# The last stores cut into shares of 117 and 11 rows, and four earlier stores into halves of 64 rows

## The chip, the cores and the metric

The kernel runs on one core of a Trainium2 chip. A core has five engines with instruction streams of their own: TensorE (PE in the profile) for matrix products, VectorE (DVE), ScalarE (ACT), GpSimd (POOL) and SyncE (SP), which issues transfers only. Data moves between the core's memory (SBUF, 128 rows called partitions) and DRAM on 16 DMA engines. The metric is the device time of one execution in microseconds, the median of several runs.

## What is computed

For 4 batches and 8 heads, keys and values are mixed over 8 blocks of 96 tokens by a matrix made doubly stochastic in five rounds; each block of queries then attends to its own mixed block. The result, 768 tokens by 512 features for each batch, goes through a gated network whose output is the kernel's output.

```python
for _ in range(5):                       # sort_net: [4, 8, 8, 8]
    P = np.exp(P - max); P /= rows(P); P /= cols(P)
k_sorted, v_sorted = P @ k_blocks, P @ v_blocks
x = softmax(q_b @ k_sorted.T / 8) @ v_sorted      # [4, 768, 512]
h = np.maximum(x @ w_in, 0.0)                     # 512 -> 1024
u, v = h[..., :512], h[..., 512:]
v_n = (v - mean) / sqrt(var + 1e-6)
v_s = einsum('ts,bsd->btd', w_spatial, v_n) + b_spatial[None, :, None]
out = (u * v_s) @ w_out                           # [4, 768, 512], float32
```

The output is 4 x 768 x 512 numbers of 4 bytes, 6.3 MB, and each batch has six tiles of 128 tokens (rows) by 512 columns.

## The kernel before

The work is cut into small units: one load, one group of matrix products with the instruction that takes the result out of PSUM, one store. The text `ORDER` (lines 18 to 51) names them one after another, and this order, written out by hand, is the order of the instructions on every engine; no scheduler moves them. A unit is a name with its arguments, and the function `u_` + name issues it. Stages of different batches are interleaved: while one batch is in its attention, the batch before it is in the gated network.

The units that matter here stand at the end of a batch.

- `OP:ps:b:n` multiplies the gated values by `w_out` for a pair of tiles, n and n+1 of batch b, into a PSUM tile (line 635). `OE:A` or `OE:D` copies the pair to a buffer `o_sb` in SBUF, on ACT (line 115) or DVE (line 117). `OS:b:n` stores the pair, 128 rows x 2 x 512, in one DMA on SP's queue (line 650).
- The last batch, b = 3, ends in smaller steps. `SH` and `GH` make the spatial product and the gate in pieces of 512 and 256 tokens (lines 665 to 678). `OH:ps:3:n:c0:c1` is the last product for one tile n and columns c0 to c1 (line 685), `OI` copies it to SBUF, and `OJ:3:n:c0:c1:S` stores it on SP's queue, or with `A` on ACT's (line 697). Tiles 2, 3, 1 and 0 are whole (512 columns), tiles 4 and 5 in column halves of 256.
- `XD:3:0` is a DMA transpose on SP's queue (line 506). It turns the first half of batch 3's attention output, and the products of line 597 read it.
- `XD`, `OS` and `OJ` on SP's queue go out in the order of the text: SP issues a DMA when its inputs are ready, and what stands behind it in the text waits.

Before the change batch 3's stores are, in the order of the text: tiles 2, 3, 4 (left half) on SP; 5 (left half) on ACT; 5 and 4 (right halves) on SP; 1 on ACT; 0 on SP. Of the earlier pairs, 1:2 and 1:4 (batch 1, tiles 2 and 4) are stored just ahead of `XD:3:0`, and 2:4, 1:0, 2:0 and 0:4 while batch 3's spatial product runs.

Copies and stores share 8 buffers (pool `ld`): a copy into a buffer waits until the store that read it last has landed. In the built program the DMAs of SP and ACT also take their completion semaphores from a set of eight, and a DMA is issued only once the DMA before it on the same semaphore has landed. The end of the program (line 807) waits for all DMAs, and then for all engines.

Of the kernel before, what the change touches and what calls it, by code (L numbers as in the profile page):

```python
# [38 lines left out]
VP:3:A:2:2:3 AT:1:3:3:1 GT:P:1:0 VP:2:A:2:0:1 ST:2:3 AT:1:3:2:1 AT:3:3:1:1 UP:0:A:2:1:1 OP:1:1:0 ST:2:0 ST:2:1 ST:2:2  # L39
OE:A:1:0 AT:2:3:0:1 LN:2:0:6 LA:2:1 UP:0:D:2:0:0 SC:1:3:0:0 LA:2:3 SC:3:3:1:0 LA:2:2 LA:2:5 LA:2:0 OP:2:1:4 AT:1:3:0:0  # L40
AT:3:3:1:0 XD:3:1 OE:A:1:4 OP:0:1:2 LA:2:4 SC:1:3:3:0 OE:D:1:2 SC:3:3:2:0 SP:2:2:2 AT:1:3:2:0 UP:0:A:2:0:1 AT:3:3:3:0
CK VP:2:A:3:4:5 GT:D:2:2 OS:1:2 SP:1:2:1 ST:3:5 OS:1:4 XD:3:0 SP:3:2:3 SP:2:2:0 ST:3:4 CF:3 GT:D:2:1 GT:P:2:3
UP:0:A:3:1:0 VP:2:D:3:2:3 VP:3:A:3:0:1 ST:3:0 ST:3:1 ST:3:2 UP:2:A:3:0:1 GT:P:2:0 LF OP:1:2:2 ST:3:3 OE:A:2:2 LN:3:0:6
OP:0:2:0 LA:3:4 LA:3:5 OS:2:2 OE:A:2:0 UP:3:D:3:1:1 LA:3:2 LA:3:0 OP:2:2:4 LA:3:3 OE:A:2:4 LA:3:1 OS:2:4 UP:0:A:3:0:0
SH:1:3:3:0 GH:P:3:3:0 SH:2:3:0:0 GH:D:3:0:0 SH:0:3:1:0 SH:2:3:2:0 SH:3:3:1:1 GH:P:3:1:0 SH:1:3:0:1 GH:P:3:2:0 OS:1:0
GH:P:3:1:1 SH:2:3:3:1 SH:3:3:2:1 OH:1:3:2:0:512:0:4 OS:2:0 GH:P:3:0:1 GH:D:3:2:1 GH:D:3:3:1 OH:2:3:3:0:512:0:4 OS:0:4
OH:0:3:4:0:256:0:4 OI:A:3:2:0:512 OI:A:3:3:0:512 OH:3:3:5:0:256:0:4 OI:D:3:4:0:256 OI:D:3:5:0:256 OJ:3:2:0:512:S
OJ:3:3:0:512:S OJ:3:4:0:256:S OJ:3:5:0:256:A OH:2:3:5:256:512:0:4 OH:1:3:1:0:512:0:4 OH:3:3:4:256:512:0:4
OI:D:3:5:256:512 OI:A:3:1:0:512 OJ:3:5:256:512:S OI:A:3:4:256:512 OJ:3:4:256:512:S OJ:3:1:0:512:A OH:2:3:0:0:512:0:4
OI:A:3:0:0:512 OJ:3:0:0:512:S  # L50
"""


# [12 lines left out]
def kernel(  # L66
# [12 lines left out]
    nc = tc.nc  # L79

    B, H, S, D = q.shape
    NB = sort_net.shape[-1]
    BLK = S // NB
    G = S // 128
# [23 lines left out]
    def queue(eng):  # L108
        if "general" in st:
            return nc.gpsimd  # L110
        return nc.scalar if eng == "A" else nc.sync

    def copy(eng, out, in_):
        if eng == "A":
            nc.scalar.copy(out=out, in_=in_)  # L115
        else:
            nc.vector.tensor_copy(out=out, in_=in_)  # L117
# [37 lines left out]
    st = {}  # L155
    count = {"e": 0, "k": 0}

    def ld_tile(name):
        return ld.tile([128, H, G * D], BF16, name=name, tag="ld")
# [197 lines left out]
    def u_QP(eng, b, hp):  # L357

        b, hp = int(b), int(hp)
        if ("qp", b) not in st:  # L360
            st["qp", b] = ld_tile("qp").rearrange("p h c -> p (h c)").rearrange(
                "p (k g h d) -> p k g h d", k=HP, g=G, h=2)
        getattr(nc, {"P": "gpsimd", "D": "vector"}[eng]).tensor_copy(
            out=st["qp", b][:, hp].rearrange("p g h d -> p h g d"),
            in_=st["q", b][:, 2 * hp:2 * hp + 2].rearrange("p h (g d) -> p h g d", g=G),
        )

    def u_QX(b, lo, hi):
# [326 lines left out]
    def u_OJ(b, n, c0, c1, eng="S"):  # L695
        b, n, c0, c1 = (int(x) for x in (b, n, c0, c1))
        queue(eng).dma_start(out=out[b, n * 128:(n + 1) * 128, c0:c1], in_=st["o1", b, n, c0])

    def u_CK():
        nc.vector.memset(bad, 0.0)  # L700
        over = lambda col, rows, in_, op, bound, test: (
            nc.vector.tensor_reduce(out=ends[0:rows, col:col + 1], in_=in_, axis=AX.X, op=op),
            nc.vector.tensor_scalar(
                out=bad[0:rows, col:col + 1], in0=ends[0:rows, col:col + 1],
                scalar1=bound, scalar2=None, op0=test),
        )
        recs = rec_all.rearrange("p n h i -> p (n h i)")
        over(0, BLK, recs, ALU.max, 1.0 / SUM_LO, ALU.is_gt)
        over(1, BLK, recs, ALU.min, 1.0 / SUM_HI, ALU.is_lt)
        over(2, BH, first[:, 0:NB], ALU.max, SUM_HI, ALU.is_gt)  # L710
        over(3, BH, first[:, 0:NB], ALU.min, SUM_LO, ALU.is_lt)
        over(4, BH, first[:, NB:2 * NB], ALU.min, COL_LO, ALU.is_lt)
# [99 lines left out]
```

## Time and profile before

| | before |
|---|---|
| median of 3 runs | 157.69 us (157.53 to 157.9) |
| the profiled execution's own time | 158.23 us |
| its span, first to last instruction | 156.4 us |
| PE busy | 147.1 us, 94% |
| DVE, ACT, POOL busy | 77%, 52%, 24% |
| granted TensorE clock | 0.999 |
| last matrix product ends | about 151.6 us into the span |

The profile gives times from the start of the span. "x" is a count of instructions. In rows of the timeline the first two numbers are start and duration; "SPq" and "ACTq" are the two engines' sequencers, which issue transfers. In a table of windows the columns are the stretch, its length, then busy time and count for PE, weight loads, DVE, ACT and POOL, then the granted clock, the mean busy share of the 16 DMA engines (1/16 is 0.06), and GB/s. A row of DMA issues gives the size and the median time from issue to landing.

### The profile page before, as it was taken

The numbers are of one execution on the slowest core, as the hardware profiler recorded it, in microseconds if no ns is written. First come the engines' busy times: TensorE is split into PE (matmuls) and PEld (weight loads), VectorE is DVE, ScalarE is ACT, GpSimd is POOL, SyncE is SP. The second block draws the span as 40 slices with busy tenths as digits, with TensorE's granted clock in tenths as the row PEclk, the third lists the DMA queues.
The fourth block names the chain that finished last, engine by engine and source line by source line (L and its number), as shares of the span: only waits on it lengthen the run. The fifth ranks groups of instructions, "written<-read, shape, count | busy, mean of one in ns | idle before, by whom it ended". The sixth has DMA issues, their size and how long they took to land.

```text
span 156.4 us, 3976 instructions
## 1 busy us (share of the span) xinstructions
PE 147.1 (94%) x1650; PEld 89.7 (57%) x1665; DVE 120.4 (77%) x270; ACT 81.5 (52%) x112; POOL 36.8 (24%) x43
## 2 busy tenths in 40 slices
PE   6998898989999999999999999999999999999970
PEld 2355776844686669557655465555565545555640
DVE  4778699849997798479898889899969796747530
ACT  3466898867889504876556034556443025540230
POOL 7923855624000040052000000400000340006500
PEclk9999999999999999999999999999999999999999
DMA  2999999999999999990026445600569300349082
GB/s 76 264 204 204 205 204 205 207 219 239 274 209 203 204 204 204 244 198 4 0 41 198 79 160 96 114 0 4 101 235 71 67 0 0 134 151 379 13 307 105
DMA packets 27653, 23.57 MB, mean 151 GB/s; under 512 B 7280, under 2 KB 24688, under 8 KB 27632
## 3 DMA queue, kind: packets, MB, share of 16 engines
q0 software_dynamic: 14352, 11.80, 47.6%
q1 hardware_dynamic: 12992, 11.10, 26.4%
q10 hardware_dynamic: 288, 0.39, 0.7%
q8 instruction: 14, 0.23, 0.6%
q14 instruction: 7, 0.06, 0.1%
HBM read 24.78 MB, written 6.29 MB: 199 GB/s over the span
## 4 chain that ended last, share of the span: by engine, by line
PE 91%; DVE 2%; ACT 2%; issue 1%; DVEq 0%; ACTq 0%
PE ps L609 15%; PE ps L597 14%; PE ps L554 13%; PE ps L635 10%; PE ps L226 7%; PE ps L488 5%; PE ps L665 5%; PE ps L442 4%; PE ps L383 4%; PE ps L314 4%; PE ps L685 3%; PE ps L410 2%; PE ps L518 2%; PE ps L531 1%; DVE kt L117 1%
## 5 line engine op out<-in xcount | busy, mean ns | idle before, releaser
L447 ACT ACTIVATE ex<-ps 96x768 bf16<-96x768 f32 x32 | 24.8, 805 | 8.7 <-PE ps L442 8.6
L625 POOL TENSOR_TENSOR gt<-z,u_sb 128x768 bf16<-128x768 f32 x6 | 9.8, 1641 | 79.0 <-DVE z L615 61.2
L609 PE MATMUL ps<-wspT,v_sb 128*128 128x384 bf16 x144 | 25.1, 326 | 0.0
L597 PE MATMUL ps<-xT,w_in_sb 128*128 128x384 bf16 x128 | 23.5, 326 | 0.0
L554 PE MATMUL ps<-w_in_sb,xT 128*128 128x512 bf16 x87 | 22.1, 380 | 1.2 <-issue 0.8
L496 DVE TENSOR_TENSOR x_sb<-ps,rec_all 96x512 bf16<-96x512 f32 x32 | 22.0, 687 | 1.1
L609 PEld LDWEIGHTS <-v_sb 128*128 128x128 bf16 x144 | 13.5, 98 | 8.9
L571 DVE BATCH_NORM_STATS2 stats<-v_sb 128x6 f32<-128x512 bf16 x24 | 16.3, 678 | 2.0 <-ACT v_sb L121 1.5
L115 ACT COPY o_sb<-ps 128x1024 f32<-128x1024 f32 (+2 forms) x12 | 9.7, 816 | 15.2 <-PE ps L685 10.2
L635 PE MATMUL ps<-w_out_sb,gt 128*128 128x512 bf16 x68 | 16.7, 379 | 0.2
L615 DVE TENSOR_TENSOR z<-ps,b_bc 128x768 f32<-128x768 f32 x12 | 11.4, 952 | 7.0 <-PE ps L609 6.8
L121 ACT ACTIVATE u_sb<-ps 128x768 bf16<-128x768 f32 x12 | 9.7, 810 | 13.1 <-PE ps L597 13.0
L597 PEld LDWEIGHTS <-w_in_sb 128*128 128x128 bf16 x128 | 11.6, 98 | 7.4
L554 PEld LDWEIGHTS <-xT 128*128 128x128 bf16 x96 | 8.6, 98 | 10.0 <-issue 1.0
L121 ACT ACTIVATE v_sb<-ps 128x1024 bf16<-128x1024 f32 (+1 forms) x9 | 8.8, 976 | 9.4 <-PE ps L554 9.4
L488 PEld LDWEIGHTS <-ex 96*128 96x128 bf16 x256 | 10.6, 97 | 3.5
L488 PE MATMUL ps<-vb,ex 96*128 96x65 bf16 x256 | 12.1, 193 | 0.0
L226 PE MATMUL ps<-warm 128*128 128x512 bf16 x35 | 10.6, 460 | 1.3 <-DVE warm L199 1.3
L635 PEld LDWEIGHTS <-gt 128*128 128x128 bf16 x72 | 6.7, 98 | 7.2
L115 ACT CAST kt<-ps 128x768 bf16<-128x768 f32 x9 | 6.9, 800 | 6.5 <-PE ps L383 6.5
L442 PE MATMUL ps<-qT,kt 64*128 64x96 bf16 x256 | 9.3, 204 | 0.5 <-DVE kt L117 0.4
L442 PEld LDWEIGHTS <-kt 64*128 64x128 bf16 x256 | 6.2, 94 | 5.8 <-issue 3.9
(94 smaller groups left out, 208.2 us busy)
## 6 DMA issues: line engine op xcount, KB each, us to landing
out_dram<-o_sb SPq DMA_DIRECT2D x9, 512.0 KB, 3.6
k_in<-in_k_dram POOLq DMA_DIRECT2D x4, 768.0 KB, 23.3
v_in<-in_v_dram POOLq DMA_DIRECT2D x4, 768.0 KB, 22.4
vb<-vm SPq DMA_DIRECT2D x24, 99.0 KB, 5.8
q_in<-in_q_dram POOLq DMA_DIRECT2D x3, 768.0 KB, 29.6
ws_in<-in_moe_w_spatial_dram POOLq DMA_DIRECT2D x2, 576.0 KB, 22.8
w_in_sb<-in_moe_w_in_dram POOLq DMA_DIRECT2D x2, 512.0 KB, 24.1
q<-in_q_dram SPq DMA_DIRECT2D x1, 768.0 KB, 4.6
```

Source lines behind the costliest of these rows:

```text
L115: nc.scalar.copy(out=out, in_=in_)
L121: nc.scalar.activation(out=out, in_=in_, func=AF.Relu)
L226: nc.tensor.matmul(t[:, 0, 0:int(w)], lhsT=warm[:, 0:128], rhs=warm[:, 0:int(w)], start=True, stop=True)
L442: nc.tensor.matmul(t[:, hh, 0:HW].rearrange("p (g x) -> p g x", g=G)[:, :, ii * TB:(ii + 1) * TB], lhsT=kT[rows, i * BLK:i * BLK + 128], r ...
L447: nc.scalar.activation(out=e_tile(b, hp, ih).rearrange("p h (x g) -> p h x g", g=G), in_=t[0:BLK, :, 0:HW].rearrange("p h (g x) -> p h x g ...
L488: nc.tensor.matmul(t[:, hh, ii * VW:ii * VW + D + 1], lhsT=e[:, c:c + 128], rhs=vb[b % 2][:, ih * NI + ii, 2 * hp + hh, 0:D + 1], start=Tr ...
L496: nc.vector.tensor_mul(out=x_sb[:, hp].rearrange("p i (h d) -> p h i d", h=2), in0=tv[:, :, :, 0:D], in1=_raw_ap(rec, 0, [rec.ap[0], [NI, ...
L554: nc.tensor.matmul(t[:, x, :], lhsT=st["xT", b][:, n // 3, kc, (n % 3) * 128:(n % 3 + 1) * 128], rhs=w_in_sb[:, kc, DH:DFF], start=(kc == ...
L571: nc.vector.bn_stats(out=stats, in_=st["v_sb", b, n])
L597: nc.tensor.matmul(t[:, x, 0:HW], lhsT=w_in_sb[:, kc, mc * 128:(mc + 1) * 128], rhs=st["xT", b][:, ih, kc, :], start=(kc == 0), stop=(kc = ...
L609: nc.tensor.matmul(t[:, x, 0:HW], lhsT=st["v_sb", b, n][:, mc * 128:(mc + 1) * 128], rhs=wspT[:, 3 * x:3 * x + 3, n, :], start=(n == 0), s ...
L635: nc.tensor.matmul(t[:, x, :], lhsT=st["gt", b, mc][:, (n0 + x) * 128:(n0 + x + 1) * 128], rhs=w_out_sb[:, mc, :], start=(mc == 0), stop=( ...
```

## The change

The matrix products, copies, loads and all other units stay as they are, and in the same order. Eight stores are cut by rows.

- `OT`, new, stores half the rows of a pair of tiles on SP's queue. The pairs 1:2, 1:4, 1:0 and 2:0 go out as rows 0 to 63 and then rows 64 to 127, at the places of their old `OS`.
- `OR`, new, stores some rows of a last tile. Tile 5 (left half, on ACT) and tile 4 (right half, on SP) go out as rows 0 to 116 and then rows 117 to 127, one behind the other on the queue they had. Of tile 1, rows 0 to 116 go out on ACT at the old place; of tile 0, rows 0 to 116 on SP at the old place, and then rows 117 to 127 of tile 0 and rows 117 to 127 of tile 1, both on ACT, end the text.
- Tiles 2 and 3, the left half of 4 and the right half of 5, and the pairs 2:2, 2:4 and 0:4, are stored as before.

In all, `out` is stored by 25 DMAs instead of 17: 20 on SP (15 before) and 5 on ACT (2 before). `u_QP`, which no unit of the text calls, is also rewritten.

```diff
-CK VP:2:A:3:4:5 GT:D:2:2 OS:1:2 SP:1:2:1 ST:3:5 OS:1:4 XD:3:0 ...
+CK VP:2:A:3:4:5 GT:D:2:2 OT:1:2:0:64 OT:1:2:64:128 SP:1:2:1 ST:3:5 OT:1:4:0:64 OT:1:4:64:128 XD:3:0 ...
...
-... GH:P:3:2:0 OS:1:0 GH:P:3:1:1 ... OS:2:0 GH:P:3:0:1 ...
+... GH:P:3:2:0 OT:1:0:0:64 OT:1:0:64:128 GH:P:3:1:1 ... OT:2:0:0:64 OT:2:0:64:128 GH:P:3:0:1 ...
...
-OJ:3:3:0:512:S OJ:3:4:0:256:S OJ:3:5:0:256:A OH:2:3:5:256:512:0:4 ...
+OJ:3:3:0:512:S OJ:3:4:0:256:S
+OR:3:5:0:256:A:0:117 OR:3:5:0:256:A:117:128 OH:2:3:5:256:512:0:4 ...
-OI:A:3:4:256:512 OJ:3:4:256:512:S OJ:3:1:0:512:A OH:2:3:0:0:512:0:4
-OI:A:3:0:0:512 OJ:3:0:0:512:S
+OI:A:3:4:256:512 OR:3:4:256:512:S:0:117 OR:3:4:256:512:S:117:128
+OR:3:1:0:512:A:0:117 OH:2:3:0:0:512:0:4 OI:A:3:0:0:512 OR:3:0:0:512:S:0:117 OR:3:0:0:512:A:117:128
+OR:3:1:0:512:A:117:128
...
+    def u_OT(b, n0, r0, r1):
+        b, n0, r0, r1 = (int(x) for x in (b, n0, r0, r1))
+        queue("S").dma_start(
+            out=out[b].rearrange("(c p) n -> p c n", p=128)[r0:r1, n0:n0 + 2, :], in_=st["o", b, n0][r0:r1])
+
+    def u_OR(b, n, c0, c1, eng, r0, r1):
+        b, n, c0, c1, r0, r1 = (int(x) for x in (b, n, c0, c1, r0, r1))
+        queue(eng).dma_start(out=out[b, n * 128 + r0:n * 128 + r1, c0:c1], in_=st["o1", b, n, c0][r0:r1])
```

More of the change, by code (lines that the diff above doesn't have):

```diff
@@ L41 @@
 AT:3:3:1:0 XD:3:1 OE:A:1:4 OP:0:1:2 LA:2:4 SC:1:3:3:0 OE:D:1:2 SC:3:3:2:0 SP:2:2:2 AT:1:3:2:0 UP:0:A:2:0:1 AT:3:3:3:0
[L42 to L49, printed above, removed]
-OI:A:3:0:0:512 OJ:3:0:0:512:S
+CK VP:2:A:3:4:5 GT:D:2:2 OT:1:2:0:64 OT:1:2:64:128 SP:1:2:1 ST:3:5 OT:1:4:0:64 OT:1:4:64:128 XD:3:0 SP:3:2:3 SP:2:2:0
+ST:3:4 CF:3 GT:D:2:1 GT:P:2:3 UP:0:A:3:1:0 VP:2:D:3:2:3 VP:3:A:3:0:1 ST:3:0 ST:3:1 ST:3:2 UP:2:A:3:0:1 GT:P:2:0 LF
+OP:1:2:2 ST:3:3 OE:A:2:2 LN:3:0:6 OP:0:2:0 LA:3:4 LA:3:5 OS:2:2 OE:A:2:0 UP:3:D:3:1:1 LA:3:2 LA:3:0 OP:2:2:4 LA:3:3
+OE:A:2:4 LA:3:1 OS:2:4 UP:0:A:3:0:0 SH:1:3:3:0 GH:P:3:3:0 SH:2:3:0:0 GH:D:3:0:0 SH:0:3:1:0 SH:2:3:2:0 SH:3:3:1:1
+GH:P:3:1:0 SH:1:3:0:1 GH:P:3:2:0 OT:1:0:0:64 OT:1:0:64:128 GH:P:3:1:1 SH:2:3:3:1 SH:3:3:2:1 OH:1:3:2:0:512:0:4
+OT:2:0:0:64 OT:2:0:64:128 GH:P:3:0:1 GH:D:3:2:1 GH:D:3:3:1 OH:2:3:3:0:512:0:4 OS:0:4 OH:0:3:4:0:256:0:4 OI:A:3:2:0:512
+OI:A:3:3:0:512 OH:3:3:5:0:256:0:4 OI:D:3:4:0:256 OI:D:3:5:0:256 OJ:3:2:0:512:S OJ:3:3:0:512:S OJ:3:4:0:256:S
+OR:3:5:0:256:A:0:117 OR:3:5:0:256:A:117:128 OH:2:3:5:256:512:0:4 OH:1:3:1:0:512:0:4 OH:3:3:4:256:512:0:4
+OI:D:3:5:256:512 OI:A:3:1:0:512 OJ:3:5:256:512:S OI:A:3:4:256:512 OR:3:4:256:512:S:0:117 OR:3:4:256:512:S:117:128
+OR:3:1:0:512:A:0:117 OH:2:3:0:0:512:0:4 OI:A:3:0:0:512 OR:3:0:0:512:S:0:117 OR:3:0:0:512:A:117:128
+OR:3:1:0:512:A:117:128
 """
@@ L362, in u_QP @@
                 "p (k g h d) -> p k g h d", k=HP, g=G, h=2)
-        getattr(nc, {"P": "gpsimd", "D": "vector"}[eng]).tensor_copy(
-            out=st["qp", b][:, hp].rearrange("p g h d -> p h g d"),
-            in_=st["q", b][:, 2 * hp:2 * hp + 2].rearrange("p h (g d) -> p h g d", g=G),
+        copy(
+            eng, st["qp", b][:, hp].rearrange("p g h d -> p h g d"),
+            st["q", b][:, 2 * hp:2 * hp + 2].rearrange("p h (g d) -> p h g d", g=G),
         )
```

## The prediction

> **What bounds the kernel now.** I began with the page's chain of work that ended last. TensorE carries it nearly throughout, and it ends in a copy of the last tile:
>
> ```profile
> PE 91%; DVE 2%; ACT 2%; issue 1%; DVEq 0%; ACTq 0%
> ...
> 146.62 4.95 PE ps L685 x30
> 151.56 0.02 issue
> 151.58 0.58 ACT o_sb L115
> ```
>
> The copy ends at 152.16, the span at 156.4. The change touches no product and no copy, so its place is mainly these 4.3 us. Second, the timelines of ACT and SP over the end, with the DMA issues of short stretches and the rows of the program's end (line 807):
>
> ```profile
> 149.16 0.40 SPq L697 DMA_DIRECT2D out_dram<-o_sb  x1
> 149.44 0.39 ACTq L697 DMA_DIRECT2D out_dram<-o_sb  x1
> 150.28 0.86 ACT L115 COPY o_sb<-ps 128x512 f32<-128x512 f32 x2 [1.59 <-PE ps L685]
> 150.90 0.34 ACTq L697 DMA_DIRECT2D out_dram<-o_sb  x1
> 151.17 0.33 SPq L697 DMA_DIRECT2D out_dram<-o_sb  x1
> 151.58 0.58 ACT L115 COPY o_sb<-ps 128x512 f32<-128x512 f32 x1 [0.44 <-PE ps L685]
> 152.19 0.33 SPq L697 DMA_DIRECT2D out_dram<-o_sb  x1
> ...
> out_dram<-o_sb SPq DMA_DIRECT2D x1, 256.0 KB, 3.3
> ...
> L807 SPq DRAIN  x3: 7/7/13, 155.5 to 155.9; - x3
> ...
> SPq L807 <- DMA out_dram<-o_sb: 1.7, 3, 1.0
> ```
>
> The last store (tile 0) is issued at 152.19 and lands 3.3 later, at 155.49. At 155.5 SP's first drain runs, and 0.93 later, at 156.43, the span ends. So the end is set by that landing. Third, the windows over these microseconds:
>
> ```profile
> 152.50:152.75 0.25, 0.00 (x0) 0.00 (x0) 0.00 (x0) 0.00 (x0) 0.00 (x0) 1.00 0.94 328
> 152.75:153.00 0.25, 0.00 (x0) 0.00 (x0) 0.00 (x0) 0.00 (x0) 0.00 (x0) 1.00 0.51 152
> 153.25:153.50 0.25, 0.00 (x0) 0.00 (x0) 0.00 (x0) 0.00 (x0) 0.00 (x0) 1.00 1.06 369
> ...
> 153.75:153.80 0.05, 0.00 (x0) 0.00 (x0) 0.00 (x0) 0.00 (x0) 0.00 (x0) 1.00 0.82 287
> 153.80:153.85 0.05, 0.00 (x0) 0.00 (x0) 0.00 (x0) 0.00 (x0) 0.00 (x0) 1.00 0.12 41
> 154.10:154.20 0.10, 0.00 (x0) 0.00 (x0) 0.00 (x0) 0.00 (x0) 0.00 (x0) 1.00 0.11 41
> 154.30:154.60 0.30, 0.00 (x0) 0.00 (x0) 0.00 (x0) 0.00 (x0) 0.00 (x0) 1.00 0.06 24
> 154.60:155.00 0.40, 0.00 (x0) 0.00 (x0) 0.00 (x0) 0.00 (x0) 0.00 (x0) 1.00 0.07 26
> 155.00:155.10 0.10, 0.00 (x0) 0.00 (x0) 0.00 (x0) 0.00 (x0) 0.00 (x0) 1.00 0.01 0
> ```
>
> The share of the DMA engines tells it. At 153.80 it falls from 0.82 to 0.12, two engines of sixteen; from 154.3 to 155.0 it is 0.06 to 0.07, one engine. So fourteen or so engines finish at 153.8, a second late one at about 154.2, and a single engine runs alone until 155.0. The store lands 0.47 after that. What made it late is in the list of queues for 151.2 to 154.2: beside the stores' rows there are packets that fetch instructions, and each sits on one engine.
>
> ```profile
> q8 instruction: 1, 0.02, 2.2%
> q14 instruction: 3, 0.02, 2.1%
> ```
>
> 2.2% of sixteen engines over 3.0 us is 1.06 us, all for one packet on one engine; the three others take 0.34 each. The late engine's lag, 155.0 less 153.8, is 1.2.
>
> **The cut of the last stores.** A store of 128 rows is spread evenly:
>
> ```profile
> DMA packets 272, 0.52 MB, mean 210 GB/s; under 512 B 16, under 2 KB 16, under 8 KB 272
> ```
>
> That is one isolated store of a pair: 256 rows of 2 KB and 16 small completion writes, 16 rows for each of 16 engines. Split evenly, 117 rows (9 x 13) need thirteen engines of 9 rows, and 11 rows eleven engines of one. I take this: with shares of 128 rows every engine has 8 rows, with 117 and 11 some eleven engines have 10, two have 9 and three have none. If the engine that ends last is among the three, its lag goes.
>
> Page "DMA: Bandwidth & Descriptors" of the Trainium skill, section "Why a DMA increments its semaphore by 16 and not by 1", says that a DMA takes the largest number up to 16 that divides its slowest dimension, and on this path the lowest-numbered engines. That gives 13 and 11 too, with 13 to 15 left empty; no row here shows engine numbers. Its "Rules for kernel authors" say to use all 16 engines; taken alone, that rule speaks for the loss in the first rival.
>
> What is late next is an ordinary engine with more rows. The price of a row is from a stretch in which only stores run:
>
> ```profile
> 115.00:116.00 1.00, 1.00 (x14) 0.71 (x13) 0.82 (x1) 0.00 (x0) 0.00 (x0) 1.00 1.01 373
> ```
>
> 373/1.01/16 is 23.1 GB/s for an engine: 0.089 us for a 2 KB row, 0.044 for 1 KB. At most all extra rows delay the end: two of 2 KB for tiles 1 and 0 each, two of 1 KB for tiles 4 and 5 each, 0.53. At least one 2 KB row, 0.09, because at 152.75 to 153.00 the engines stand half idle (0.51) and take up what came earlier. I take three rows, 0.27: both of tile 0, and tile 1's one that is issued last. Nearer to the low end, as that gap shows. Data then ends at 153.80 + 0.27 = 154.07 instead of 155.02, so 0.95 sooner.
>
> **The added issues.** ACT's second DMA for tile 5 takes 149.83 to about 150.18, ahead of the copy that waits for PE until 150.28: hidden by 0.1, and were it late, the next copy still waits 0.44 for PE. SP's second for tile 4 goes 151.50 to 151.83, ahead of the one at 152.19: hidden by 0.36. At the end ACT is free: tile 0's 11 rows are issued at about 152.19, tile 1's at 152.52. Tile 1's must wait, by the eight semaphores, for tile 5's first share, whose like in the trace lands 3.2 after 149.44:
>
> ```profile
> out_dram<-o_sb ACTq DMA_DIRECT2D x1, 128.0 KB, 3.2
> out_dram<-o_sb SPq DMA_DIRECT2D x1, 128.0 KB, 2.0
> ```
>
> That is 152.64. Tile 0's data began about 0.8 after its issue (0.51, then 1.06 in the windows), so these rows move from about 153.45, for 0.1, and are in by 154.07. SP's 117 rows of tile 0 wait for tile 4's left half, 149.16 + 2.0 = 151.2: nothing. Price of the issues: nothing; if the cover is short, a tenth.
>
> **The halves of 64 rows.** The same bytes, in twice as many DMAs. SP's issues took 0.90 for two before the transpose; four may take 1.8, until 115.8, ahead of 117.92. Their pace is the question. At the pace of whole stores nothing changes. The slow bound is the nearest rows of which each DMA reads few SBUF rows, the moves of 16 rows each of batch 3:
>
> ```profile
> 97.00:99.00 2.00, 2.00 (x27) 1.16 (x25) 1.97 (x4) 1.13 (x2) 0.00 (x0) 1.00 0.90 160
> ...
> 113.98 0.90 SPq L650 DMA_DIRECT2D out_dram<-o_sb  x2
> 117.92 1.44 SPq L506 DMA_TRANSPOSE xT<-x_sb  x1
> ...
> 117.00:118.00 1.00, 0.95 (x5) 0.47 (x5) 0.97 (x4) 0.59 (x1) 0.00 (x0) 1.00 0.70 254
> 118.00:119.00 1.00, 1.00 (x8) 0.50 (x6) 0.92 (x5) 0.30 (x1) 0.00 (x0) 1.00 0.00 0
> ...
> xT<-x_sb SPq DMA_TRANSPOSE x1, 5.3
> ...
> 124.54 1.47 PE L597 MATMUL ps<-xT,w_in_sb 128*128 128x384 bf16 x8
> ```
>
> 160/0.90 against 373/1.01 is 0.48 of the pace. The two pairs, 1.05 MB from 114.9 to 117.7, would then run until 120.8, 1.8 into the transpose, whose packets start at about 119. It lands at 123.2; 125.0 would be 0.5 after line 597 wants it. So the price is 0 to 0.5 and I take 0: even half the slowdown (0.9) fits into the 1.3 of slack. For 1:0 and 2:0, bounds 0 and 3.0 us of DMA time; they share a block issued from 138.32, and
>
> ```profile
> 145.00:145.50 0.50, 0.50 (x7) 0.46 (x5) 0.35 (x1) 0.00 (x0) 0.50 (x1) 1.00 0.15 45
> 148.00:148.50 0.50, 0.50 (x7) 0.44 (x6) 0.00 (x0) 0.39 (x1) 0.00 (x0) 1.00 0.00 0
> ```
>
> its data is through by 145.1, while tile 2's begins after 148.5: 3.4 of cover. Price 0.
>
> A rule that speaks against the halves is on page "SBUF — State Buffer" of the Trainium skill, "Door 1: The DMA port swizzle": rows 0 to 63 reach only 8 of 16 ports, so a half moves at about half pace. By it the transpose lands near 125.0 and the sum loses at most 0.5 of its gain; by the whole stores' pace it loses nothing.
>
> **The sum.** -0.95 for the late engine, 0 for issues and halves. The profiled execution took 158.23 with a span of 156.4; its 158.23 would become 157.28. It stands 0.54 above the median of 157.69, and the end is in every execution, so the median becomes 156.74.
>
> **Rivals.**
> First, slower: the engine that ends last is one of the first eleven. Then it carries ten rows, not eight, behind the same fetch. It is behind by then and has no gap to fill, so 0.27 to 0.53 are added: 158.0 to 158.2, say 158.1. It decides at the eleventh engine. For it: eleven of sixteen places, if places were drawn at random. Against it: only two engines are late after 153.8, the split spares three, and if each stream of instructions has its fixed engine, these may well be neighbours at one end of the numbering. I lean to the far end; no row settles it. The skill's page on DMA ("Latency and other measured facts") calls engines 7 and 15 the usual slow ones, which is one on each side.
> Second, no change: the shares don't empty the late engine, because it is the twelfth or thirteenth (nine rows for eight, 0.09 to 0.27) or because 117 rows are dealt unevenly over all sixteen. 157.7 to 157.9.
> Third, the halves run at half pace and the transpose holds TensorE by 0.5: 157.24 beside the gain. The slack of 1.3 speaks against it.
>
> **How the numbers follow.** Forecast 0.58, own range 156.5 to 157.3: low with one extra row and the runs' spread, high if the second late engine (154.2) stays loaded. First rival 0.26, second 0.10, third 0.06. A measurement can tell 0.2%, about 0.32 us, from no change: faster is below 157.37, which takes the forecast, and most of the third, 0.62; same 0.11, slower 0.27. The range is 156.4 to 158.1, which leaves out the upper part of the first rival.
>
> **What would show it.** Right: after the issue of tile 0's 117 rows the landing of the last DMA is near 154.5, the drain of line 807 follows, and no stretch of 0.06 lasts 0.7 us. Stores of 117 rows show 13 completion writes. Wrong: a single busy engine to 155 or later (first rival), line 597 near 124.5 waiting for `xT` (third), or a share as uneven as before (second). It also fails if the fetch moves with the added instructions.

## The result and the profile after

| | before | changed |
|---|---|---|
| median of 5 runs each | 157.69 us (157.53 to 157.9) | 158.22 us (158.12 to 158.52) |
| ratio to before | | 1.0040 (1.0024 to 1.0056) |
| the traced execution's own time, span | 158.23, 156.4 | 158.12, 156.3 |

The change makes the kernel slower by 0.53 us; the forecast was 0.95 less. The two traced executions have nearly the same span, because TensorE ended at different times in them. TensorE's last step in the chain of waits of the changed kernel, start and length:

```profile
146.10 4.95 PE ps L687 x30
```

It ends at 151.05, where before it was 151.57. This end moved between 150.8 and 151.6 over all the traces here. In this pair the 0.5 is there from 33 us on, far ahead of the first store that was changed. So from here on times at the end are counted from the end of ACT's last copy (152.17 before, 151.65 after), with a plus sign. From there to the end of the span it is 4.26 before and 4.67 after: 0.41 more, close to the 0.53 of the medians.

The timeline of ACT and SP over the end of the changed kernel (two stretches):

```profile
148.92 0.98 ACTq L708 DMA_DIRECT2D out_dram<-o_sb  x2
150.00 0.86 ACT L117 COPY o_sb<-ps 128x512 f32<-128x512 f32 x2 [1.83 <-PE ps L687]
150.89 0.76 SPq L708 DMA_DIRECT2D out_dram<-o_sb  x2
151.07 0.58 ACT L117 COPY o_sb<-ps 128x512 f32<-128x512 f32 x1 [0.20 <-PE ps L687]
151.68 0.30 ACTq L708 DMA_DIRECT2D out_dram<-o_sb  x1
...
152.21 0.33 SPq L708 DMA_DIRECT2D out_dram<-o_sb  x1
152.37 0.30 ACTq L708 DMA_DIRECT2D out_dram<-o_sb  x1
```

Tile 5's two shares hold ACT for 0.98 (the first alone 0.64; the whole store took 0.39 before). The next copy starts later, so that the last copy waits only 0.20 for TensorE instead of 0.44. SP issues tile 4's two shares from 150.89, and tile 0's 117 rows only at 152.21, +0.56; before it was +0.03. Between 151.66 and 152.12 SP stands still, and no row names what for. The last issue, tile 1's 11 rows, is at 152.37, +0.72: ACT waits on the semaphore of tile 5's first share, whose last landing comes at 152.35.

The windows of the changed kernel (columns as before: the last two are the share of the 16 DMA engines and GB/s):

```profile
152.50:152.75 0.25, 0.00 (x0) 0.00 (x0) 0.00 (x0) 0.00 (x0) 0.00 (x0) 1.00 0.85 299
153.25:153.50 0.25, 0.00 (x0) 0.00 (x0) 0.00 (x0) 0.00 (x0) 0.00 (x0) 1.00 0.71 238
154.00:154.25 0.25, 0.00 (x0) 0.00 (x0) 0.00 (x0) 0.00 (x0) 0.00 (x0) 1.00 0.41 148
154.25:154.50 0.25, 0.00 (x0) 0.00 (x0) 0.00 (x0) 0.00 (x0) 0.00 (x0) 1.00 0.13 49
154.50:154.75 0.25, 0.00 (x0) 0.00 (x0) 0.00 (x0) 0.00 (x0) 0.00 (x0) 1.00 0.07 25
154.75:155.00 0.25, 0.00 (x0) 0.00 (x0) 0.00 (x0) 0.00 (x0) 0.00 (x0) 1.00 0.03 8
```

Two things differ from before. The share is 0.85 at most from 152.50 on, where before it reached 0.94 to 1.06, and it stays up for longer: before it fell to 0.12 at +1.64, here it is still 0.41 at +2.35 to +2.60. And there is again one engine alone (0.07), until 154.90. Data ends at +3.25 instead of +2.86. The last landing is at +3.70 instead of +3.28.

The end of the program is a list. SP waits for one completion semaphore after the other in a fixed order, four others first and then the eight that SP's and ACT's DMAs share. A wait that is met already takes 0.06. These are SP's rows of the program's last line, before (line 807, from 154.6 to 155.5) and after (line 818, from 154.3 to 155.42):

```profile
L807 SPq EVENT_SEMAPHORE  x3: 28/28/28, 154.7 to 155.5; - x3
```

```profile
L818 SPq EVENT_SEMAPHORE  x6: 28/28/28, 154.4 to 155.4; - x6
```

After, six waits end 0.18 to 0.24 apart (+2.71, 2.92, 3.16, 3.35, 3.53, 3.71 in the trace's events), each with the last landing of another share: tile 1's 117 rows, tile 4's 117 and 11, tile 0's 11 and 117, tile 1's 11. In each of these six DMAs one landing comes 0.3 to 1.2 after all others of that DMA. The three late ones of the 11-row shares can only come from one of the eleven engines that count for them; so here a late engine is among the eleven. The records of single packets show its rows: from +2.43 to +3.16 it moves nine rows of tile 0, one straight behind the other, and then one row of tile 1. So it has ten rows of a tile and not eight.

The halves, in the windows that answer to those of the prediction:

```profile
115.00:116.00 1.00, 1.00 (x8) 0.58 (x6) 0.97 (x3) 0.00 (x0) 0.00 (x0) 1.00 0.98 197
118.00:119.00 1.00, 1.00 (x8) 0.61 (x7) 0.86 (x8) 0.82 (x1) 0.00 (x0) 1.00 0.77 234
```

At the same share of busy engines (0.98 against 1.01) they move 197 GB/s where whole stores moved 373, 0.53 of the pace, and they run past 118. The timeline of SP and PE there:

```profile
117.41 2.00 SPq L508 DMA_TRANSPOSE xT<-x_sb  x1
...
117.98 6.01 PE L611 MATMUL ps<-wspT,v_sb 128*128 128x384 bf16 x36
124.02 1.15 PE L599 MATMUL ps<-xT,w_in_sb 128*128 128x384 bf16 x6
```

Line 599 follows the block before it without an idle mark: the transpose is still in time.

### The profile page after: what moved, and what is told of

Read it like the earlier page. It is cut to its first block, busy times and chain, and to the rows that moved or that the text cites. A ratio compares the mean times of both kernels' runs of the same rounds, so it can differ in the third digit from the quotient of the medians.

```text
span 156.3 us, 3986 instructions
## 1 busy us (share of the span) xinstructions
PE 147.2 (94%) x1650; PEld 89.8 (57%) x1665; DVE 120.5 (77%) x270; ACT 81.5 (52%) x112; POOL 36.8 (24%) x43
## 4 chain that ended last, share of the span: by engine, by line
PE 83%; DMA 8%; ACT 2%; POOL 1%; issue 1%; DVE 1%; ACTq 0%; POOLq 0%
PE ps L611 15%; PE ps L599 14%; PE ps L556 13%; PE ps L637 10%; DMA v_in<-in_v_dram 8%; PE ps L490 5%; PE ps L667 5%; PE ps L444 4%; PE ps L385 4%; PE ps L687 3%; PE ps L316 3%; PE ps L412 2%; PE ps L520 2%; PE ps L533 1%; PE ps L403 1%
```

## The experiments

Times are medians; each ratio is to the kernel before, run beside it (157.66 to 157.74 in all of these).

**The two halves of the change.** The first leaves the pairs whole and cuts the last stores; the second does the opposite.

```diff
-OT:1:2:0:64 OT:1:2:64:128 ... OT:1:4:0:64 OT:1:4:64:128 ... OT:1:0:0:64 OT:1:0:64:128 ... OT:2:0:0:64 OT:2:0:64:128
+OS:1:2 ... OS:1:4 ... OS:1:0 ... OS:2:0
```

```diff
-OR:3:5:0:256:A:0:117 OR:3:5:0:256:A:117:128
+OJ:3:5:0:256:A
-OR:3:4:256:512:S:0:117 OR:3:4:256:512:S:117:128
+OJ:3:4:256:512:S
-OR:3:1:0:512:A:0:117
+OJ:3:1:0:512:A
-OR:3:0:0:512:S:0:117 OR:3:0:0:512:A:117:128
-OR:3:1:0:512:A:117:128
+OJ:3:0:0:512:S
```

> Only the last four stores are cut into shares of 117 and 11 rows; the four pairs are stored whole, as before the change. Theory A: the loss comes from the end, because the engine that ends last is one of the first eleven and carries ten rows for eight, or because the last DMA is issued 0.5 to 0.7 us later after the last copy. Then this kernel is as slow as the changed one, 0.4 to 0.6 us over the kernel before, about 158.2. Theory C: the halves of 64 rows cost it. Then this one is at the time before, 157.7, or, if my forecast of the tail was right after all, near 156.7.

> Only the four pairs are stored in halves of 64 rows; the last tiles are stored whole. Theory A: no change, 157.5 to 157.9, because the halves lie under products that do not wait for them. Theory C (halves run at about half pace and something behind them is late): 0.3 to 0.6 us slower, about 158.2. In the windows between 114 and 120 us the share of the DMA engines should stay near 1 with clearly fewer GB/s than the 373 of whole stores, whichever theory holds, if the halves are slow at all.

Measured: the shares alone 158.57, 1.0052 (1.0039 to 1.0065), the halves alone 157.85, 1.0014 (1.0003 to 1.0024). So the loss is in the shares, and it is more than the 0.4 to 0.6 that was expected. But the two do not add up: 0.87 and 0.15 over the 157.70 beside them make 1.02, and both together cost 0.53. Something in the halves gives back what the shares cost. The list above is what does it, as shown further down.

**The fetch that makes an engine late.** These leave out the careful path for large values (its branch and the hint), and so the instructions that are fetched near the end.

```diff
-        with tc.If(st["beyond"] > 0, preferred_fallthrough_block=True, label="general"):
-            general_path()
...
-XT:1:D:1:1:0 LA:0:0 BH LA:0:4
+XT:1:D:1:1:0 LA:0:0 LA:0:4
```

> The kernel before without the second, careful path and the branch to it (it is not entered for these inputs, so the output is unchanged; the flag is still computed and read). It tests whether the fetches of instructions near the end make one engine late. If they belong to the branch, the packets of queues q8 and q14 after 151 us go, no single engine runs alone after 154, the last store lands about 2.1 us after its issue and not 3.3, and the time falls by 0.7 to 1.2 us, to about 156.7. If the fetches come in any case (the program is read ahead in blocks), nothing changes beyond 0.3.

> The changed kernel without the careful path and the branch. Theory A with rows on the late engine: without fetches no engine is late, and what is left of the loss is the extra rows of the ordinary engines, 0.1 to 0.5 over the kernel before without the branch. Theory B, later issues of the last DMAs: the loss against the kernel before without the branch is 0.5 to 0.8, larger than with the branch, because on the ordinary engines the last DMA is issued 0.7 later after the last copy and nothing hides that.

> The kernel before without the unit BH, which marks the branch over the careful path as likely for three engines. If the fetch of 1.05 us on one engine during the last stores comes from that mark, it moves: earlier, and the lag at the end shrinks (down to 156.8, as without the branch), or later, behind a stop of TensorE that nothing at the end waits for. If not, 157.6 to 157.9.

Measured: before without it 156.81, 0.9945 (0.9931 to 0.996); the changed kernel without it 158.08, 1.0023 (1.0014 to 1.0033); the hint alone away 157.80, 1.0012 (1.0002 to 1.0021). In the first the packet of 1 us is gone from the end, no engine is left behind, data ends at +1.69 and the span 3.46 after the copy instead of 4.26. The prediction's reading of before holds: a fetch makes an engine late. The last landing is 1.17 sooner without it (+2.11 instead of +3.28). The time shows only 0.89 of that, because without the careful path the stretch from SP's first drain to the end of the span takes 1.27 instead of 0.90.

With nothing to gain from an empty engine, the change costs 1.27 (158.08 against 156.81), more than either theory allowed. Its windows, with the copy's end at 151.85:

```profile
153.60:153.85 0.25, 0.00 (x0) 0.00 (x0) 0.00 (x0) 0.00 (x0) 0.00 (x0) 1.00 0.84 303
154.35:154.60 0.25, 0.00 (x0) 0.00 (x0) 0.00 (x0) 0.00 (x0) 0.00 (x0) 1.00 0.11 41
154.60:154.85 0.25, 0.00 (x0) 0.00 (x0) 0.00 (x0) 0.00 (x0) 0.00 (x0) 1.00 0.02 8
```

Data ends at +2.88 instead of +1.69. That is no sooner than the +2.86 of the kernel before with its late engine, and SP's first drain comes at +3.37, where before it was +3.36. So by this run the changed kernel would gain about nothing even if no engine were late. Taking the hint away moves the fetch of 1 us, from -0.23 to -0.94, but not the time.

**Which engine is late.** Against the shares alone, one kernel cuts all four tiles by columns, into the same number of DMAs, so that all 128 rows are in each, and one into shares of 120 and 8 rows. These are the edits at tile 0; tiles 1, 4 and 5 are cut alike:

```diff
-OR:3:0:0:512:S:0:117 OR:3:0:0:512:A:117:128
+OC:3:0:0:512:S:0:448 OC:3:0:0:512:A:448:512
```

```diff
-OR:3:0:0:512:S:0:117 OR:3:0:0:512:A:117:128
+OR:3:0:0:512:S:0:120 OR:3:0:0:512:A:120:128
```

A third cuts tile 0 alone, against before:

```diff
-OJ:3:0:0:512:S
+OR:3:0:0:512:S:0:117 OR:3:0:0:512:A:117:128
```

> The kernel with only the last stores cut (158.57 as measured), but each is cut by columns: all 128 rows and 448 of 512 columns, then 64 columns (192 and 64 of 256). The DMAs are as many, on the same queues, in the same order; but every engine has its even share of rows. Theory A, uneven rows: the loss goes for the most part, time 157.7 to 158.0. Theory B, more DMAs, later issues and their waits: the loss stays, 158.4 to 158.7. Half and half would be near 158.2.

> As the kernel with only the last stores cut, but in shares of 120 and 8 rows. Split evenly, 120 rows need 15 engines of 8 rows, and 8 rows 8 engines of one: the first eight carry 9 rows, one of sixteen none. The DMAs, their order and their waits stay. Theory A: the extra rows are halved (one for two) and nearly the full number of engines works, so at least half of the 0.87 lost goes: 157.8 to 158.2. Theory B: 158.4 to 158.6.

> Only the very last store, tile 0, is cut into 117 rows on SP and 11 on ACT; all else as before the change. Both go out right after the last copy, so no DMA is issued later and no engine's queue holds one more ahead of it. Theory A with the late engine among the first eleven: two more rows at the end of its queue, 0.17, time 157.8 to 157.9. If the late engine were one of the three that get no rows of it: 8 rows of 0.08 to 0.09 less on it, 0.6 to 0.7 sooner, about 157.0. Theory B: within 0.1 of the kernel before.

Measured: by columns 158.90, 1.0077 (1.0064 to 1.0091); 120 and 8 rows 158.24, 1.0041 (1.0024 to 1.0059); tile 0 alone 158.25, 1.0036 (1.0022 to 1.005).

The cut by columns is slower than both theories had it, and it tells nothing of engines: SP's DMA of 64 columns of tile 4 took 1.54 to issue (three take 2.40), so tile 0's went out 1.1 late.

```profile
150.73 2.40 SPq L712 DMA_DIRECT2D out_dram<-o_sb  x3
```

With 120 and 8 rows one of the 8 landings of tile 5's small share comes 0.9 after the others, as one of the 11 does in the changed kernel: a late engine is among the eight that it uses. The runs of this kernel fall into two groups, four from 158.06 to 158.24 and three from 158.70 to 158.88, and the trace is of the second (158.78). So the median says little about whether fewer extra rows cost less.

Tile 0 alone shows what the prediction had hoped for, in its windows and in SP's list of waits (line 817, from 154.45 to 154.93):

```profile
153.25:153.65 0.40, 0.00 (x0) 0.00 (x0) 0.00 (x0) 0.00 (x0) 0.00 (x0) 1.00 0.89 307
153.85:154.05 0.20, 0.00 (x0) 0.00 (x0) 0.00 (x0) 0.00 (x0) 0.00 (x0) 1.00 0.20 77
154.05:154.45 0.40, 0.00 (x0) 0.00 (x0) 0.00 (x0) 0.00 (x0) 0.00 (x0) 1.00 0.00 0
```

```profile
L817 SPq EVENT_SEMAPHORE  x8: 27/28/28, 154.5 to 154.9; - x8
```

The copy ends at 151.86. No engine runs alone: data ends at +2.16, 0.70 sooner than before, and the 117 rows have landed at +2.59. Tile 1, stored whole, still has landings at +2.22 and tile 4 at +2.55, so the late engines are there, but the landings show none that holds rows of tile 0. Then SP needs from +2.60 to +3.09 for eight waits. The 117 rows are on the first semaphore of the eight, and the waits behind it come one after the other, though they are met. That gives back 0.43 of the 0.70. And the runs that were timed without a trace (158.05 to 158.47) do not even show the rest; the traced execution took 157.64.

**The same again.** Three further traces of tile 0 alone, and tile 0 alone without the careful path:

> The same kernel as the one with only tile 0 cut (117 and 11 rows), for a second profile of one execution. The first profile showed no engine running alone after the rest (157.64, data through 2.2 us after the last copy), while the other runs took up to 158.47. Theory M: the engine that a fetch delays is not the same in every execution; then a second profile will more often than not show a lone engine on the last stores, its span about 156.4 to 156.7. Theory F: the late engine is always one of the three that get no rows of tile 0; then this profile looks like the first, span 155.8, and the spread of the times has another cause, such as TensorE's own end moving.

> A third profile of the same kernel, only tile 0 cut. Theory M: over the looks, spans fall into two groups, one near 155.8 without and one near 156.4 to 156.7 with a lone engine until 3 us or more after the last copy. Theory F: span 155.8 again.

> A fourth profile of the same kernel, only tile 0 cut. As for the third: two groups by theory M, one group near 155.8 by theory F.

> Only tile 0 cut into 117 and 11 rows, and the careful path with its branch taken out, so that no fetch delays an engine during the last stores. It measures by itself what the uneven shares cost, with the last DMA issued as early as before: theory A's extra rows are 0.09 to 0.27 over the 156.81 of the kernel before without the branch, 156.9 to 157.1. If it is 0 the shares are free and the whole loss of the changed kernel without the branch (1.27) is from later issues; if it is 0.4 or more, the 13 engines read their nine rows more slowly than sixteen read eight.

Measured: 157.86, 157.50 and 157.75 for the traced executions, data ending at +2.18 to +2.20 in each; so the empty late engine is no accident of one trace. Without the careful path 157.89 (157.76 to 158.4), 1.08 more than before without it. The windows of before without the careful path (copy's end 151.62), then with tile 0 cut (151.64):

```profile
152.60:153.00 0.40, 0.00 (x0) 0.00 (x0) 0.00 (x0) 0.00 (x0) 0.00 (x0) 1.00 1.00 379
153.20:153.40 0.20, 0.00 (x0) 0.00 (x0) 0.00 (x0) 0.00 (x0) 0.00 (x0) 1.00 0.22 51
153.40:153.80 0.40, 0.00 (x0) 0.00 (x0) 0.00 (x0) 0.00 (x0) 0.00 (x0) 1.00 0.00 0
```

```profile
152.60:153.00 0.40, 0.00 (x0) 0.00 (x0) 0.00 (x0) 0.00 (x0) 0.00 (x0) 1.00 0.79 225
153.20:153.40 0.20, 0.00 (x0) 0.00 (x0) 0.00 (x0) 0.00 (x0) 0.00 (x0) 1.00 0.70 266
153.40:153.80 0.40, 0.00 (x0) 0.00 (x0) 0.00 (x0) 0.00 (x0) 0.00 (x0) 1.00 0.27 87
```

Here no engine is late, and the price of the shares stands alone. The share is 0.79, about 13 of 16 (0.81), instead of 1.00. And the engines that work are slower at first: from 152.60 to 153.00, 225 GB/s at 0.79 is 17.8 for each busy engine, where 379 at 1.00 is 23.7. Why they slow down, no run shows. Data ends at +2.27 instead of +1.69: 0.58 for tile 0 alone. The landing follows, +2.70 instead of +2.12, and the list adds 0.44. Both make 1.02 of the 1.08.

**The list of waits.** One cuts an early pair in two and nothing else: this moves tile 0's whole store from the last to the first of the eight semaphores. The others are tile 0 cut with both shares on SP (the 117 rows last in the list, the 11 rows first), tile 0 cut as before once more, and tile 0 cut with seven early pairs in halves, which brings the 117 rows to the end of the list.

The first, against before:

```diff
-OS:1:2
+OT:1:2:0:64 OT:1:2:64:128
```

The second, against tile 0 cut alone; in the fourth the edit above is made for 1:2, 1:4, 1:0, 2:0, 2:2, 2:4 and 0:2 beside tile 0's shares:

```diff
-OR:3:0:0:512:S:0:117 OR:3:0:0:512:A:117:128
+OR:3:0:0:512:S:0:117 OR:3:0:0:512:S:117:128
```

> Before, with the pair 1:2 alone stored in two halves of 64 rows, 40 us ahead of the end. The one added DMA moves every later one to the next of the eight semaphores; tile 0's store gets the first of them and not the eighth. Theory of the list: the landing of tile 0 is near 3.3 after the last copy as before, and SP's seven waits behind it take 0.43, so the time is 0.4 to 0.5 above before: 158.1 to 158.2. Rival: where a semaphore stands in the list makes no difference, and one pair in halves costs nothing, as four pairs cost 0.16: 157.7.

> Before, with tile 0 alone stored as 117 and 11 rows, both on SP's queue. The 117 rows then use the eighth completion semaphore, on which SP's list of waits at the end closes, as the whole tile 0 does before, and the 11 rows the first. Theory of the list: when tile 0 alone is cut, with the 11 rows on ACT, the 117 rows land 2.6 after the last copy instead of 3.3, but their semaphore is the first of eight in the list, and the seven waits behind it take 0.43. With both on SP the list must end within 0.15 of the last landing, at about 2.75 after the copy instead of 3.09, the span from the end of the last copy 3.6 to 3.7 (before 4.26), and the time 0.4 to 0.6 under the kernel before: 157.1 to 157.3. Rival: the list costs nothing and something outside of the trace holds the time; then the time is that of tile 0 cut with 11 rows on ACT, 157.7 to 158.3.

> Before, with tile 0 alone stored as 117 rows on SP and 11 rows on ACT, once more, timed beside the other two. Its four traces so far have 0.27 to 0.16 less from the last copy to the end of the span than before, but the five timed runs had a median of 158.25 against 157.69, and four single looks 157.50 to 157.86. By the traces: 157.4 to 157.6. If the timed runs are right and the traces fall short of them: 158.2.

> Before, with tile 0 alone in 117 rows on SP and 11 on ACT, and seven earlier pairs (1:2, 1:4, 1:0, 2:0, 2:2, 2:4, 0:2) in halves of 64 rows. The seven added DMAs move the 117 rows from the first place in SP's list of waits at the end to the last. By the list, 0.43 of the 3.99 from the last copy to the end of the span goes, if the 117 rows land last: 3.5 to 3.6 in the trace. For the time there are two theories. If the timed executions go as the traces of tile 0 cut alone do (landing 2.6 after the copy), the time is 0.6 to 0.7 under before: 157.0 to 157.1. If in the timed executions a late engine still holds rows of tile 0, landing near 3.3 as before, which with the list's 0.43 makes the 158.2 measured for tile 0 alone, the time is that of before: 157.6 to 157.8.

Measured: 158.11, 1.0036 (1.0023 to 1.0048) for one pair in halves; 158.08, 1.004 (1.0025 to 1.0055) for both shares on SP; 158.20, 1.0031 (1.002 to 1.0043) for the repeat, in which the traced execution took 157.48; 157.67, 1.0 (0.999 to 1.0011) with the 117 rows at the list's end.

One more DMA, 40 us ahead of the end, costs 0.44, and four cost 0.15 (the halves alone, with four waits behind the late one). This is the list, as forecast. It is also why shares and halves do not add up: with the shares alone 0.26 pass from the last landing (+3.82) to the end of the list (+4.08), and with the halves beside them 0.01. SP's rows of the line, with one pair in halves (154.83 to 155.3) and with the 117 rows last (153.5 to 154.63):

```profile
L817 SPq EVENT_SEMAPHORE  x8: 28/28/28, 154.8 to 155.3; - x8
```

```profile
L817 SPq EVENT_SEMAPHORE  x4: 28/28/28, 153.9 to 154.6; - x4
L817 SPq DRAIN  x3: 7/7/13, 154.7 to 155.0; - x3
```

In the first the eight waits run off one behind the other after the landing. In the second the last wait ends with the landing and the drain follows 0.07 later. With both shares on SP my forecast failed: the 117 rows were last in the list, but the 11 rows, first in it, landed last of all (+3.21), and seven waits followed again. One of their eleven landings comes 0.69 after the other ten, so here a late engine holds rows of tile 0 again, though only the queue of the 11 rows has changed.

The last of the four also bears on the timed runs: to put the store at the end of the list, with seven pairs in halves, gave 0.53 (158.20 to 157.67) and no more. That is the second of the two theories. In the timed executions tile 0 cut into shares gains nothing by itself, while in every traced execution of the whole program data ended 0.3 to 0.7 sooner. What differs between them is in no trace, and stays open.

**The late issue.** In the changed kernel tile 0's 117 rows go out at +0.56. Here tile 4's 11 rows stand behind them on SP, and the changed kernel runs beside it once more.

```diff
-OI:A:3:4:256:512 OR:3:4:256:512:S:0:117 OR:3:4:256:512:S:117:128
+OI:A:3:4:256:512 OR:3:4:256:512:S:0:117
...
-OR:3:1:0:512:A:117:128
+OR:3:1:0:512:A:117:128 OR:3:4:256:512:S:117:128
```

> The changed kernel with tile 4's 11 rows moved behind tile 0's 117 rows on SP's queue, so that tile 0's 117 rows are issued within 0.1 of the end of the last copy, as in before, and not 0.56 after it. Theory of the loaded engine: an engine that an instruction fetch has put behind carries 10 rows of each cut tile, and the end comes when it has worked off its rows, whatever the time at which tile 0 is issued; the last landing stays about 3.7 after the copy and the time that of the changed kernel, 158.1 to 158.3. Theory of the late issue: the 0.53 of delay on SP is what the changed kernel loses; the time falls to 157.6 to 157.8.

> The changed kernel once more, beside the run with tile 4's share moved: 158.1 to 158.3, and in its trace six late landings one after another, as in its first trace, if the late engine is the same in every execution.

Measured: 158.28, 1.0039 (1.0026 to 1.0053), beside 158.34, 1.0044 (1.0026 to 1.0061). Tile 0's 117 rows went out at +0.16, in the first of these two issues, and tile 4's 11 rows behind them:

```profile
151.80 0.74 SPq L708 DMA_DIRECT2D out_dram<-o_sb  x2
```

The windows of the same kernel, whose copy ends at 151.64:

```profile
153.25:153.50 0.25, 0.00 (x0) 0.00 (x0) 0.00 (x0) 0.00 (x0) 0.00 (x0) 1.00 0.48 139
154.25:154.50 0.25, 0.00 (x0) 0.00 (x0) 0.00 (x0) 0.00 (x0) 0.00 (x0) 1.00 0.45 172
154.75:155.00 0.25, 0.00 (x0) 0.00 (x0) 0.00 (x0) 0.00 (x0) 0.00 (x0) 1.00 0.03 8
```

An issue 0.40 sooner gains nothing: tile 0's 117 rows have landed at +3.50 instead of +3.52, and data ends at +3.21 instead of +3.25. In the shares alone these rows even went out at +0.06, and data ended at +3.30. So the late issue is not the loss. The repeat of the changed kernel shows the six late landings again, 0.2 to 1.1 after the others, with data until +3.23. But it is not simply one loaded engine either: at 154.25 to 154.50, +2.6 to +2.9, seven engines are still at work here, and at 153.25 the share is 0.48 where thirteen engines would give 0.81. Why the ordinary engines go slower when tile 0's share is out sooner, the runs do not say.

None of the kernels with the full computation was faster than the kernel before.

## Why the prediction was wrong

*What bounds the kernel before.* Right. The end is set by the last landing, and an engine that a fetch has put behind makes it 1.17 later, close to the lag of 1.2 that the prediction read: that is what goes away with the fetch.

*Where the rows go.* Right: the 117-row stores have 13 completion counts of their own and the 11-row stores 11, with the rest of the sixteen counted at once.

*"If the engine that ends last is among the three, its lag goes."* This is the first step that failed, and the one that made the kernel slower. In the changed kernel the engine that ends last gets rows of every share, so the first rival held: 158.0 to 158.2 was its time, 158.22 came out, and its added 0.27 to 0.53 was 0.39 in the trace's data. I gave it 0.26. With tile 0 alone cut, the 11 rows on ACT, the late engine was among the three in all five traces; with both shares on SP it was not. That the fetch's packet falls on another engine when instructions change, as the prediction's last sentence feared, would explain all of them; no row shows engine numbers, so it is argued and not shown. The Trainium skill's page "DMA: Bandwidth & Descriptors", section "Rules for kernel authors", asks for all 16 engines, and the runs side with it: a store of 117 rows alone, with no late engine about, cost 0.58 of data time.

*"I take three rows, 0.27."* This step failed too, and alone it takes the whole gain. For all four tiles the term was 1.19 without a late engine (+2.88 instead of +1.69), and for tile 0 alone 0.58, above even the upper bound of 0.53, which was meant for four tiles. I had priced rows on an engine that goes on at its own pace; what happened with tile 0 alone is that three engines did nothing and the others moved 17.8 GB/s each instead of 23.7 at first. The other 0.61 comes with the shares of the three other tiles and tile 0's later issue; no run without a late engine parts these. So an empty late engine would have brought about nothing: the lag of 1.2 away, 1.19 added.

*"Price of the issues: nothing."* The sizes failed: ACT's first DMA of 117 rows took 0.64 and not 0.39, tile 0's rows left at +0.56 and tile 1's at +0.72. The price held as far as the runs with a late engine tell: an issue 0.40 sooner moved the time by 0.06.

*What the sum left out: the order of SP's waits.* I counted DMAs for what they issue and move, but not for the semaphore that they pass on to those behind them. In the changed kernel this costs nothing, since eight more DMAs bring the last ones back to the list's end. It is worth 0.44 with seven waits behind the last landing, as one pair in halves shows. Tile 0's cut lost 0.43 of its traced 0.70 there.

*The halves.* Half pace was there (197 against 373 GB/s; 64 rows reach half the ports, says the page "SBUF — State Buffer" of the Trainium skill, "Door 1: The DMA port swizzle", and this trace agrees with 0.53), and the slack in front of line 599 hid it, as forecast. What they cost alone, 0.15, is of the size of the four waits behind the late landing (0.25 in the trace).

## What to carry to other kernels

A program's end is a chain of its own: last landing, a list of waits in fixed order, drains. When DMAs are added anywhere, look up which completion semaphore the last store gets and how many waits stand behind it. To starve a late DMA engine of rows, first find out whether it is still the same engine after the change. And measure what the uneven shares cost without any late engine: here it was 1.19, as much as could be won.

## What was not expected of the hardware

- One more DMA at 115 us cost 0.44 at 157 us: SP takes 0.06 for each wait that is met already, and seven stood behind the last landing.
- A packet of instructions, 16 KB, holds one DMA engine for 0.95 to 1.37, and that engine's lag stays until the last store: without it the last landing is 1.17 sooner.
- One DMA of 128 rows by 64 columns took SP 1.54 to issue; three of that shape on ACT took 0.34 to 0.62, and those of 256 columns on SP take 0.33 to 0.40.
- Traced and timed executions of one kernel can differ by 0.7 at the end (with tile 0 cut, 157.48 to 157.86 traced, and 158.05 to 158.49 for all timed ones but one), where for the kernel before they agree once TensorE's end is taken into account.
